# Folded weights interleaved on their way into PSUM, plain copies out, and a new order of all queues

## The chip, the cores and the metric

The kernel runs on one core of a Trainium2 chip. The time is that of one execution in microseconds of device time. A core has five queues of instructions that run side by side and wait for each other through semaphores: TensorE (PE, the matrix engine; its weight loads are shown as PEld), VectorE (DVE), ScalarE (ACT), GpSimd (POOL) and SyncE (SP, which here only issues DMAs).

## The reference

One block of a transformer on a sequence of 2048 rows of 448 numbers, in bf16: a linear attention with 16 heads of 28, then a gated feed forward with 1792 hidden units. Cut to what matters:

```python
x = A_x
xn = layernorm(x)
q, k, v = split_heads(xn @ wqkv)                  # 16 heads of 28
pq, pk = q @ w_phi[h], k @ w_phi[h]               # a 28x28 matrix per head
phi_q = concat(softmax(pq), softmax(-pq))
phi_k = concat(softmax(pk), softmax(-pk))
kv = phi_k.T @ v;  z = phi_k.sum(rows)
o  = (phi_q @ kv) / (phi_q @ z + 1e-6)
h  = x + heads_together(o) @ wo
hn = layernorm(h)
out = h + (sigmoid(hn @ w_gate) * (hn @ w_up)) @ w_down
```

## The kernel before

**Folding.** q is only used as q @ w_phi, and k as k @ w_phi. So the kernel multiplies the weights first: Wq2 = Wq @ w_phi and Wk2 = Wk @ w_phi, and projects the normalised rows with these. `fold(w, banks)` does it, with w = 0 for the keys and w = 1 for the queries, in four row tiles kt of 128 rows. One tile (`w2m0_0` to `w2m0_3`, `w2m1_0` to `w2m1_3`) is four matmuls of 112 columns, one for each group of four heads; together they fill 448 columns of a PSUM bank. `Wphi` holds w_phi as block diagonals, so that the columns of a group come out as head by head, 28 each. A copy (`w2e0_..`, `w2e1_..`) takes the bank to SBUF as bf16, on ACT or DVE. The key weights are transposed first on TensorE (`wT0` to `wT3`, taken out by `wTe0` to `wTe3`); the query weights arrive transposed by DMA (`ld_q0` to `ld_q3`).

**Interleaving.** Behind the projections, the sum over the 28 numbers of a head (`ss`, DVE) and the product with its reciprocal (`phi`) work on pairs of heads whose numbers alternate: number d of head 0, number d of head 1, number d+1 of head 0, and so on. The kernel before brings the weights' columns into this order in the copy: `w2e0` reads the bank with the two heads of a pair swapped to the innermost place, as one instruction of 448 columns, and `w2e1` does so in two instructions of 224 columns each, which also leave 8 columns of padding behind each 56.

**Stages.** The rows are 16 tiles t of 128. The loads `x0`, `x1`, `x2`, ... bring one or two tiles each. Statistics (`bst`, `agg`, DVE), the reciprocal root (`pow1`, POOL) and the normalisation (`xn`, on POOL, DVE or ACT) follow. The first four tiles are transposed on TensorE (`xT0` to `xT3`, copies `xT0e` to `xT3e`), the others by DMA from SP. Then:

- Key projections of the first four tiles `ppa0 ppb0 ppa2 ppb2` and value projections `vva0 vvb0 vva2 vvb2`, then both together for each further tile, `pva4 pvb4` to `pva15 pvb15`. Each is a pair: the contraction runs in two halves of 64 rows of the array that work at the same time, one on each of two banks, and in the b part the halves change banks. A b part that writes what its a part has just written waits for the end of the a part, and the order puts short items in between.
- `ek` (exponentials, two on ACT), `ss`, `rs` (reciprocal), `phi` (POOL or DVE), `v1` (the value copy, ACT or DVE), and the products `kva`, `kvb` of all 16 tiles, which add up in banks 6 and 7. `kvzA` to `kvzD` take them out.
- Query projections `pqa`, `pqb` for four chunks of 512 rows, exponentials `eq` on ACT.
- For each tile the numerator `num` (banks 6 and 7 again), and on DVE `rsm`, `qq`, `b`, `c`, `rden`; the division `o`; a transpose `oT`, on TensorE for tiles 0 and 1 and by DMA for the rest; the output projection (`wof0`, `wof1`, then `woa`, `wob` for two tiles at once); the residual `h` and the second normalisation (`bs2`, `ag2` or `nm`, `sq`, `ve`; `pow2`; `hn`) and its transpose `hT`, again on TensorE for tiles 0 and 1 (copies `hT0e`, `hT1e`).
- The feed forward in groups of 2, 2, 4, 4 and 4 tiles: gate and up `ga`, `gb` for each of 14 column tiles (256 columns for the first two groups, 512 for the others), the sigmoid `sig`, for some a copy `uc` of the up part (ACT), the product `hh` (DVE or POOL), and the down projections `dn`, `dp` in pairs of tiles, `dm`, `dl` for the last four. `fin` adds the residual, `out` stores.

Before the projections, TensorE runs matmuls on zeros (`warm0` to `warm9`).

**The order.** `ORDER` holds the whole order of all five queues, written out as names. The semaphores follow from the reads and writes that each item states: an item waits for the last writer of what it reads, and for the readers of what it overwrites. Each queue is worked off strictly in order. `PACE` holds back two loads until certain items are done. An item with a choice of engines runs on the engine in whose list it stands. Through the helper that records them most matmuls stand under line 333 in the profile, the fold's under 619, copies out of PSUM under 538, the query copies under 636.

Of the kernel before, what the change touches and what calls it, by code (L numbers as in the profile page):

```python
# [18 lines left out]
class Graph:  # L19
# [109 lines left out]
    def emit(self, nc):  # L129
# [133 lines left out]
    ),  # L263
# [86 lines left out]
def build(nc, A_x, A_wqkv, A_w_phi, A_wo, B_w_gate, B_w_up, B_w_down, out):  # L350
# [10 lines left out]
    with ExitStack() as es:  # L361
# [68 lines left out]
        def B(i):  # L430
            return ("bank", i)
# [180 lines left out]
        def fold(w, banks):  # L612
            for kt in range(KT):
# [3 lines left out]
                def mm(e, kt=kt, b=b, r0=r0):  # L617
                    for gg in range(G):
                        p = e.matmul(bk(b)[:, gg * GP:(gg + 1) * GP], lhsT=WT[w][:GP, gg, r0:r0 + P], rhs=Wphi[:, gg, :],  # L619
                                     start=True, stop=True)  # L620
                    return p
# [409 lines left out]
```

## Time and profile before

| | |
|---|---|
| median of 3 runs | 202.40 us (202.32 to 202.81) |
| the profiled execution | 202.64 us, its span 200.7 us |
| TensorE busy | 195.7 us (98%) |
| DVE / ACT / POOL busy | 129.1 / 100.0 / 64.5 us |
| granted TensorE clock | 1.0 |
| DMA | 16.25 MB moved, HBM read 8.34 MB |

The profile is one execution. Busy time of an engine is the union of its instructions; matmuls are pipelined and overlap, so the time from one start to the next is shorter than a duration. The timeline's rows give start, time covered, engine, line, output and inputs, and in brackets the idle time before, with what ended it. What lies between the span and the time of the execution (1.9 us) is outside the program's instructions.

### The profile page before, as it was taken

How to read it: one execution, taken by the hardware profiler on the slowest of the kernel's cores; microseconds unless marked ns; L12 is line 12 of the kernel's file. 1: busy time of each engine (PE TensorE's matmuls, PEld its weight loads, DVE VectorE, ACT ScalarE, POOL GpSimd, SP SyncE). 2: the span in 40 equal slices, each digit the busy share in tenths (PEclk: the TensorE clock that was granted, in tenths of full speed). 3: DMA queues.
4: the chain of work that ended last, by engine and by line, in shares of the span. 5: the costliest groups of instructions: out<-in, count | busy, mean ns of one | idle time of the engine just before them, and what ended most of it. 6: DMA issues, size and time to landing. Idle time of an engine off the chain costs nothing.

```text
span 200.7 us, 5879 instructions
## 1 busy us (share of the span) xinstructions
PE 195.7 (98%) x2500; PEld 115.2 (57%) x2500; DVE 129.1 (64%) x317; ACT 100.0 (50%) x215; POOL 64.5 (32%) x101
## 2 busy tenths in 40 slices
PE   7999999999989999999999999999999999999995
PEld 2945555666568878786444444555555555554443
DVE  6899999979899874445759877346332422272224
ACT  3778997998795874444342432324323212222220
POOL 5599989713534854560050110001400000000000
PEclk9999999999999999999999999999999999999999
DMA  6964442669997330221006320020212000004002
GB/s 163 311 143 99 83 82 52 178 200 285 322 188 96 78 57 9 46 56 31 0 10 117 78 45 11 20 60 23 56 49 54 0 0 3 0 0 140 0 0 91
DMA packets 32866, 16.25 MB, mean 81 GB/s; under 512 B 25096, under 2 KB 31944, under 8 KB 32840
## 3 DMA queue, kind: packets, MB, share of 16 engines
q1 hardware_dynamic: 32336, 15.86, 33.9%
q8 instruction: 19, 0.31, 0.6%
q10 hardware_dynamic: 504, 0.03, 0.2%
q14 instruction: 7, 0.06, 0.1%
HBM read 8.34 MB, written 1.84 MB: 51 GB/s over the span
## 4 chain that ended last, share of the span: by engine, by line
PE 97%; DVE 1%; issue 0%
PE psum L333 85%; PE psum L952 5%; PE psum L531 3%; PE psum L545 1%; PE psum L619 1%; PE psum L894 1%; PE psum L606 1%; DVE b_sb L810 0%; DVE c_sb L813 0%; PE psum L892 0%; DVE xnT L538 0%; DVE x_sb L959 0%; DVE zero L438 0%; DVE rsm L807 0%; DVE qq L808 0%
## 5 line engine op out<-in xcount | busy, mean ns | idle before, releaser
L333 PE MATMUL psum<-xnT,wg_sb 64*128 64x512 bf16 (+1 forms) x490 | 93.2, 333 | 0.1
L333 PE MATMUL psum<-xnT,wu_sb 64*128 64x512 bf16 (+1 forms) x490 | 92.7, 333 | 0.0
L919 ACT ACTIVATE sg_sb<-psum 128x512 bf16<-128x512 f32 (+1 forms) x70 | 35.5, 515 | 76.7 <-PE psum L333 76.1
L925 DVE TENSOR_TENSOR hhT<-sg_sb,psum 128x512 bf16<-128x512 bf16 (+1 forms) x44 | 28.9, 672 | 46.8 <-ACT sg_sb L919 46.5
L333 PEld LDWEIGHTS psum<-xnT,wg_sb 64*128 64x128 bf16 x490 | 44.5, 94 | 21.1 <-DVE hhT L925 2.2
L333 PEld LDWEIGHTS psum<-xnT,wu_sb 64*128 64x128 bf16 x490 | 44.5, 94 | 12.6
L333 PE MATMUL psum<-wd_sb,hhT 64*128 64x448 bf16 x336 | 37.0, 349 | 0.0
L333 PEld LDWEIGHTS psum<-wd_sb,hhT 64*128 64x128 bf16 x336 | 17.9, 94 | 14.2 <-DVE x_sb L845 0.5
L333 PE MATMUL psum<-wv_sb,xnT 64*128 64x448 bf16 x112 | 22.2, 351 | 0.1
L333 PE MATMUL psum<-Wk,xnT 64*128 64x448 bf16 x112 | 22.0, 350 | 0.1
L692 POOL TENSOR_TENSOR phi<-hhT,rs 128x896 bf16<-128x896 bf16 x10 | 17.6, 1765 | 2.5 <-DVE rs L688 2.1
L682 DVE TENSOR_REDUCE ss<-hhT 128x32 f32<-128x896 bf16 x16 | 17.2, 1073 | 0.5 <-ACT hhT L679 0.2
L854 POOL TENSOR_SCALAR ve<-ssq 128x1 f32<-128x1 f32 x11 | 2.7, 243 | 45.9 <-ACT junk L851 45.5
L730 ACT ACTIVATE eq<-psum 120x1024 bf16<-120x1024 f32 x16 | 15.6, 1029 | 1.4 <-PE psum L333 1.2
L333 PE MATMUL psum<-xnT,Wq 64*120 64x512 bf16 x112 | 14.9, 384 | 0.1
L819 POOL TENSOR_TENSOR o_pad<-c_sb,rden 128x448 bf16<-128x448 bf16 x10 | 9.3, 936 | 14.0 <-DVE rden L815 13.9
L924 ACT CAST xn_pad<-psum 128x256 bf16<-128x256 f32 x26 | 9.5, 378 | 5.6 <-PE psum L333 5.6
L959 DVE SCALAR_TENSOR_TENSOR x_sb<-psum,x_sb 128x448 bf16<-128x448 f32 (+2 forms) x17 | 9.4, 592 | 3.9 <-PE psum L333 2.1
L333 PE MATMUL psum<-wo_o,oT 64*128 64x448 bf16 x49 | 11.5, 349 | 0.0
L333 PE MATMUL psum<-wo_e,oT 64*128 64x448 bf16 x49 | 11.5, 349 | 0.0
L952 PE MATMUL psum<-wd_sb,hhT 128*128 128x448 bf16 (+2 forms) x70 | 11.1, 316 | 0.0
L333 PEld LDWEIGHTS psum<-Wk,xnT 64*128 64x128 bf16 x112 | 7.7, 94 | 5.3 <-issue 1.3
(113 smaller groups left out, 258.0 us busy)
## 6 DMA issues: line engine op xcount, KB each, us to landing
out_dram<-x_sb SPq DMA_DIRECT2D x15, 112.0 KB, 1.9
x_sb<-in_A_x_dram SPq DMA_DIRECT2D x7, 224.0 KB, 4.2
wd_sb<-in_B_w_down_dram SPq DMA_DIRECT2D x7, 224.0 KB, 5.5
wg_sb<-in_B_w_gate_dram SPq DMA_DIRECT2D x3, 448.0 KB, 5.5
wu_sb<-in_B_w_up_dram SPq DMA_DIRECT2D x3, 448.0 KB, 7.0
wv_sb<-in_A_wqkv_dram SPq DMA_DIRECT2D x2, 224.0 KB, 4.6
wk_sb<-in_A_wqkv_dram SPq DMA_DIRECT2D x2, 196.0 KB, 3.7
wo_e<-in_A_wo_dram SPq DMA_DIRECT2D x1, 336.0 KB, 3.0
```

The source lines that it names most:

```text
L333: p = e.matmul(o, lhsT=w, rhs=r, start=st, stop=sp, tile_position=(row, 0))
L531: p = e.matmul(bk(3)[:, 0:size], lhsT=zero[:, 0:P], rhs=zero[:, 0:size], start=True, stop=True)
L682: op("dve", "ss%d" % t, lambda e: e.tensor_reduce(ss[:, s, :].rearrange("p (b h) -> p b h", h=2), eks.rearrange("p b (d h) -> p b h d", h= ...
L692: return e.tensor_tensor(phi[:, sp, :, :, :].rearrange("p b a n -> p (b a) n")[:, :, 0:56].rearrange("p b (d h) -> p b d h", h=2), eks.rea ...
L730: op("act", "eq%d_%d%s" % (c, i, "pm"[sg]), lambda e, sg=sg: e.activation(eq[c][:, sg, 2 * i:2 * i + 2, :].rearrange("p g n -> p (g n)"), ...
L819: return e.tensor_tensor(o_pad[:, t % NO, off:off + D].rearrange("p (h d) -> p h d", h=H), c_sb[:, t % NS, :, 0:DH], rden[:, t % NS, :][:, ...
L854: op(("pool", "dve"), "ve%d" % t, lambda e: e.tensor_scalar(ve2[:, t:t + 1], ssq2[:, t:t + 1], 1.0 / D ** 3, EPS, op0=ALU.mult, op1=ALU.ad ...
L919: op("act", "sig" + nm, lambda e: e.activation(sg_sb[:, k, 0:N], bk(bg)[:, 0:N], ACT.Sigmoid), r=[B(bg)], w=[("sg", k)])
L924: op("act", "uc" + nm, lambda e: e.copy(up, bk(bu)[:, 0:N]), r=[B(bu)], w=[ub])
L925: op(("pool", "dve") if nm in UCOPY else "dve", "hh" + nm, lambda e: e.tensor_tensor(hhT[(t0 // 4) % NHH][:, ff, ns], sg_sb[:, k, 0:N], up ...
L952: p = e.matmul(bk(b)[:, lo:hi], lhsT=hb[:, ff, TS(t)], rhs=wd_sb[:, ff, lo:hi], start=ff == 0, stop=ff == FT - 1)
L959: op("dve", "fin%d%s" % (t, nm), lambda e: e.scalar_tensor_tensor(out=h_sb[:, t, lo:hi], in0=bk(b)[:, lo:hi], scalar=1.0, in1=h_sb[:, t, l ...
```

## The change

The fold's matmuls write their 112 columns with a step of two PSUM words: head 0 and head 1 of a pair are interleaved as they are written, and the moving operand is read in its stored order. Each copy then moves its bank in order, in one instruction, for keys and queries alike; only the padding of the query weights' target is left as a step. The columns that end up in SBUF are the same as before.

All five lists of `ORDER` are new. In SP's list `x12` stands ahead of three of the four query loads, `x14` one transpose later, `ld_wd3` ahead of `oT2` and `oT3`, `ld_wd4` to `ld_wd6` behind `oT7`. From DVE to ACT go `w2e0_1`, `w2e1_0` and `oT0e`, so that all eight weight copies are ACT's; from ACT to DVE go `xT2e`, `v1_4` and `h1`. DVE and POOL exchange products (`phi`, `hh`, `o`) and small items. On TensorE all items are there as before, in another order.

```diff
     "sp": (
-        "x1 x0 ld_k0 x2 ld_k2 x4 x6 ld_v0 x10 ld_v2 x8 ld_q2 ld_q1 ld_q0 x12 ld_q3 xT4 xT5 x14 xT6 ...
+        "x1 x0 ld_k0 x2 ld_k2 x4 x6 ld_v0 x10 ld_v2 x8 x12 ld_q1 ld_q2 ld_q0 ld_q3 xT4 xT5 xT6 x14 ...
-        "... ld_wd0 ld_wd1 ld_wd2 oT2 oT3 ld_wd3 ld_wd4 ld_wd5 ld_wd6 oT5 oT4 oT7 oT6 oT8 hT2 hT3 ...
+        "... ld_wd0 ld_wd1 ld_wd2 ld_wd3 oT2 oT3 oT4 oT5 oT6 oT7 ld_wd4 ld_wd5 ld_wd6 hT3 hT2 oT8 ...
     "act": (
-        "... wTe1 wTe0 xT1e xT0e w2e0_0 w2e0_2 w2e0_3 nm1_4 xT2e ek0 ek1 v1_0 par v1_1 ek2 w2e1_1 v1_2 v1_3 ek3 ...
+        "... wTe0 wTe1 xT1e xT0e w2e0_0 w2e0_2 w2e0_3 w2e0_1 nm1_4 ek1 ek0 nm1_6 v1_1 v1_0 ek2 nm1_8 w2e1_0 v1_2 ek3 ...
     "pe": (
-        "warm0 wT1 wT0 warm1 xT1 warm2 warm3 xT0 w2m0_0 wT2 wT3 warm4 warm5 w2m0_2 w2m0_1 w2m0_3 warm6 warm7 warm8 "
-        "ppa0 xT2 ppb0 xT3 warm9 vva0 vvb0 ppa2 seed ppb2 vva2 w2m1_1 vvb2 kvb0 w2m1_0 w2m1_3 pva4 kva0 kvb1 pvb4 "
+        "warm0 wT0 wT1 xT1 warm1 warm2 warm3 xT0 warm4 wT2 wT3 w2m0_0 warm5 w2m0_2 w2m0_1 w2m0_3 warm6 warm7 warm8 "
+        "warm9 ppa0 ppb0 vva0 xT3 xT2 vvb0 ppa2 seed ppb2 vva2 w2m1_0 vvb2 w2m1_2 w2m1_1 pva4 kva1 pvb4 pva5 kva0 "
...
-        "kvb15 kva14 pqa1_1 qs wwo num0 pqb1_1 num1 pqa2_0 num2 pqb2_0 pqa2_1 oT0 pqb2_1 num3 oT1 wof0 wof1 num4 "
-        "pqa3_0 pqb3_0 pqa3_1 num5 pqb3_1 hT0 hT1 wgu num6 ga0_1 ga0_0 gb0_1 gb0_0 woa2 num7 ga0_3 ga0_2 gb0_3 gb0_2 "
-        "wob2 num8 ga0_5 ga0_4 gb0_5 gb0_4 woa4 ga0_7 ...
+        "kvb14 kva15 pqa1_1 qs pqb1_1 wwo num0 pqa2_0 num1 pqb2_0 num2 pqa2_1 oT0 pqb2_1 pqa3_0 num3 oT1 wof0 wof1 "
+        "num4 pqb3_0 pqa3_1 pqb3_1 hT0 hT1 wgu num5 ga0_1 ga0_0 gb0_1 gb0_0 woa2 num6 ga0_3 ga0_2 gb0_3 wob2 gb0_2 "
+        "ga0_5 num7 gb0_5 ga0_4 gb0_4 ga0_7 ...
-        "wob12 gb4_10 ga4_13 dn4_0 ga4_12 gb4_13 gb4_12 dn4_4 ga8_1 ...
+        "wob12 gb4_10 ga4_13 gb4_13 ga4_12 dn4_0 gb4_12 dn4_4 ga8_1 ...
     "dve": (
-        "... bst1 agg1 bst0 xn1 agg0 xn0 bst3 bst2 agg3 wTe2 wTe3 agg2 bst5 w2e0_1 bst4 agg5 ... xT3e agg7 agg11 agg10 ss0 ...
+        "... bst1 agg1 bst0 agg0 xn1 xn0 bst3 bst2 agg3 wTe2 agg2 wTe3 bst4 bst5 nm1_2 bst7 agg5 ... xT3e xT2e ss1 bst8 ...
-        "... bs2_0 rden3 ag2_0 rsm4 bs2_1 qq4 ag2_1 b4 c4 hn0 hn1 rsm5 qq5 b5 hT0e c5 hT1e rden5 rsm6 ...
+        "... bs2_0 rden3 bs2_1 rsm4 ag2_0 ag2_1 qq4 h1 b4 hn0 hn1 c4 hT0e hT1e rden4 rsm5 qq5 b5 c5 rden5 ...
...
                 def mm(e, kt=kt, b=b, r0=r0):
                     for gg in range(G):
-                        p = e.matmul(bk(b)[:, gg * GP:(gg + 1) * GP], lhsT=WT[w][:GP, gg, r0:r0 + P], rhs=Wphi[:, gg, :],
+                        p = e.matmul(bk(b)[:, gg * GP:(gg + 1) * GP].rearrange("p (c d h) -> p c h d", c=2, h=2),
+                                     lhsT=WT[w][:GP, gg, r0:r0 + P], rhs=Wphi[:, gg, :].rearrange("p (c h d) -> p c h d", c=2, h=2),
                                      start=True, stop=True)
                     return p
...
                 if w == 0:
-                    dst = W2[0][:, kt, :].rearrange("p (c d h) -> p c h d", c=8, h=2)
-                    src = bk(b)[:, 0:D].rearrange("p (c h d) -> p c h d", c=8, h=2)
-                    evac("w2e%d_%d" % (w, kt), dst, src, B(b), ("W2", w, kt))
+                    dst, src = W2[0][:, kt, :], bk(b)[:, 0:D]
                 else:
                     dst = W2[1][:, kt, :, :].rearrange("p g (a n) -> p a g n", a=2)[:, :, :, 0:56]
-                    src = bk(b)[:, 0:D].rearrange("p (a g h d) -> p a g d h", a=2, g=G, h=2)
-
-                    def cp(m, dst=dst, src=src):
-                        def f(e):
-                            for a in range(2):
-                                p = m(e)(dst[:, a].rearrange("p g (d h) -> p g d h", h=2), src[:, a])
-                            return p
-                        return f
-                    op(("act", "dve"), "w2e%d_%d" % (w, kt), (cp(lambda e: e.copy), cp(lambda e: e.tensor_copy)), r=[B(b)], w=[("W2", w, kt)])
+                    src = bk(b)[:, 0:D].rearrange("p (a g n) -> p a g n", a=2, g=G)
+                evac("w2e%d_%d" % (w, kt), dst, src, B(b), ("W2", w, kt))
```

98 rows, old and new, of the table ORDER are left out of this document.

## The prediction, made before the changed kernel was run

> **What bounds the kernel now.** I read the busy shares first, then the chain that ended last, then the busy time by stretch, then the order of time around the two places where the stretches differ.
>
> ```profile
> span 200.7 us, 5879 instructions
> PE 195.7 (98%) x2500; PEld 115.2 (57%) x2500; DVE 129.1 (64%) x317; ACT 100.0 (50%) x215; POOL 64.5 (32%) x101
> PEclk9999999999999999999999999999999999999999
> PE 97%; DVE 1%; issue 0%
> ```
>
> TensorE (PE) is busy for 195.7 of 200.7 us at full granted clock, and the chain of waits is 97% TensorE. So this is a kernel whose end is the sum of TensorE's stream. The change adds and removes no matmul of the work, so it can move the time in three ways only: an earlier start of the stream, fewer or more holes in it, and matmuls that take longer. The stretches say where holes are left:
>
> ```profile
> 10.00:15.00 5.00, 4.94 (x51) 2.19 (x52) 4.98 (x16) 3.57 (x9) 4.89 (x10) 1.00 0.66 144
> 25.00:30.00 5.00, 5.00 (x76) 2.76 (x74) 5.00 (x10) 4.64 (x11) 4.41 (x5) 1.00 0.41 82
> 50.00:60.00 10.00, 8.98 (x144) 5.74 (x142) 9.14 (x29) 8.53 (x11) 4.10 (x6) 1.00 1.14 253
> 80.00:120.00 40.00, 40.00 (x531) 23.47 (x528) 26.22 (x71) 16.98 (x44) 10.38 (x19) 1.00 0.24 47
> ```
>
> The columns are the stretch, its length, then busy time of PE, PEld, VectorE (DVE), ScalarE (ACT), GpSimd (POOL). Visible holes: the start, 1.02 us in 50 to 60, the tail. From 80 to 120 there is none, so nothing done there on ACT, DVE or POOL can be gained. VectorE is as full as TensorE in 25 to 30: two engines go side by side, and work that leaves one of them does not shorten the stretch.
>
> **The copies out of PSUM.** These are the three kinds of copy, by line (min/median/max ns):
>
> ```profile
> L538 ACT CAST v<-psum x15: 535/541/604, 14.1 to 40.5; 128x448 bf16<-128x448 f32 x15
> L538 ACT CAST Wk<-psum x3: 662/664/664, 7.7 to 9.1; 128x448 bf16<-128x448 f32 x3
> L538 DVE CAST Wk<-psum x1: 641/641/641, 8.9 to 8.9; 128x448 bf16<-128x448 f32 x1
> L636 ACT CAST Wq<-psum x6: 346/377/401, 16.8 to 21.4; 128x224 bf16<-128x224 f32 x6
> ```
>
> The interleaving copy of a key weight costs 664 ns on ACT, a copy of the same size whose source is in order (the value tile v) 541; so the key copies (w2e0) lose 0.12 each. A query copy (w2e1) is two halves of 377, becomes one, and loses about 0.2. All eight now run on ACT, those of w2e0_1 and w2e1_0 and oT0e come from DVE, and DVE takes xT2e, v1_4 and h1 in return (copies of 0.4 to 0.6). That is nearly a swap for DVE, and worth time only where a copy is waited for: the start.
>
> ```profile
> 5.79 0.97 ACT L538 COPY WkT<-psum 112x448 bf16<-112x448 bf16 x2 [0.80 <-PE psum L606]
> 6.70 1.14 ACT L538 COPY xnT<-psum 128x512 bf16<-128x512 bf16 x2
> 7.74 0.66 ACT L538 CAST Wk<-psum 128x448 bf16<-128x448 f32 x1
> 8.57 1.19 ACT L538 CAST Wk<-psum 128x448 bf16<-128x448 f32 x2 [0.17 <-PE psum L619]
> 9.98 0.93 PE L333 MATMUL psum<-Wk,xnT 64*128 64x448 bf16 x8
> 10.85 0.40 PE L545 MATMUL psum<-ident,xn_pad 128*128 128x128 bf16 x4
> 11.18 0.74 PE L333 MATMUL psum<-Wk,xnT 64*128 64x448 bf16 x6
> 11.85 0.40 PE L545 MATMUL psum<-ident,xn_pad 128*128 128x128 bf16 x4
> 12.29 1.74 PE L333 MATMUL psum<-wv_sb,xnT 64*128 64x448 bf16 x14
> 13.95 0.93 PE L333 MATMUL psum<-Wk,xnT 64*128 64x448 bf16 x8
> 14.71 0.36 PE L716 MATMUL psum<-epsr,epsl 64*128 64x232 bf16 x2
> 17.46 0.97 ACT L538 CAST v<-psum 128x448 bf16<-128x448 f32 x2
> 18.14 0.35 PE L333 MATMUL psum<-Wk,xnT 64*128 64x448 bf16 x1
> ```
>
> The last key copy ends at 8.57 + 1.19 = 9.76 and the first projection (ppa0) starts at 9.98, 0.22 later. In the new order ACT makes four plain copies in a row. Two in a row take 0.97 (the row at 17.46), so they start 0.43 apart; from 7.74 the fourth starts at 9.03, ends at 9.57, and ppa0 starts at 9.79: **0.2 earlier**. What covers this is that the second normalised tile is ready sooner (agg0 stands ahead of xn1 on DVE) and wT2, wT3 ahead of the first fold on TensorE; without that cover the copies stretch as now and the gain is nothing.
>
> **The first pairs.** The b half of a pair writes the bank of its a half, so it waits for a's end unless something stands between. The 14 matmuls at 12.29 are vva0 and vvb0 with nothing between: 0.93 + 0.74 is nearly 1.74, so vvb0 starts 1.00 after vva0. With a filler the next item starts 0.76 after (13.95 to 14.71): a bare pair costs 0.24. Transposes in between cost 0.87 to enter (9.98 to 10.85), 0.33 for four. Now: ppa0, xT2, ppb0, xT3, vva0, vvb0, 3.97 from 9.98 to 13.95. New: ppa0 ppb0 bare 1.00, ppb0 0.57 (0.67 from 11.18 to 11.85, less the 0.11 that entering a transpose costs more), vva0 0.87, xT3 and xT2 together 0.33 + 0.22, vvb0 0.57: 3.56. But ppa2 needs both transposes evacuated, both now on DVE: xT3 starts 2.44 after ppa0, its copy starts about 0.43 later, two copies take 0.76, hand-over 0.12: 3.75. So **0.2 more** is gained, not 0.4.
>
> Then pva4 at 18.14 waits for the value copy, 17.46 + about 0.54 = 18.0. Everything ahead is 0.4 earlier, the query copy before it shorter, but its place behind ek2 and nm1_8 on ACT stays: I take 0.3. In return kvb0, 0.2 of TensorE, is not done yet by then. Left: 0.15.
>
> **18 to 43 us.** I take nothing. Both orders have four pairs with only one short kv item between (pva9, 11, 12, 14 now; pva4, 11, 12, 13 then), one place where two kv items of different halves meet, and three places where fold matmuls enter. TensorE has no hole to close, and DVE exchanges four phi products against four with POOL.
>
> On SP the load of x12 goes ahead of three weight transposes:
>
> ```profile
> 6.04 3.81 SPq L507 DMA_TRANSPOSE WqT<-in_A_wqkv_dram  x3
> 9.90 0.58 SPq L434 DMA_DIRECT2D x_sb<-in_A_x_dram  x1
> 10.53 1.12 SPq L507 DMA_TRANSPOSE WqT<-in_A_wqkv_dram  x1
> 16.38 0.37 PE L619 MATMUL psum<-Wphi,WqT 112*128 112x112 bf16 x4
> 51.40 4.70 SPq L832 DMA_TRANSPOSE oT<-o_pad  x2
> ```
>
> x12 starts 3.8 us earlier, three transposes 0.6 later, the fourth where it was (10.53), and its reader starts at 16.38: covered. x12's statistics move up with it on DVE, and nobody waited for them. Behind it, ld_wd3 is put ahead of oT2 and oT3, whose issue ends at 56.10, while their reader woa2 stands behind num5 or num6 and two gate/up items, past 58.4; and ld_wd4 to 6 go behind oT7, while their first reader dn0_8 stands behind nearly all gate/up items of the first two tiles. I take both at nothing; if that cover is gone the price is one more load's time, about 0.5.
>
> **43 to 59 us, the hole.**
>
> ```profile
> 43.84 1.24 DVE L759 TENSOR_TENSOR kvz<-psum,mask 64x232 bf16<-64x232 f32 x3 [1.06 <-PE psum L333]
> 45.19 0.41 PE L333 MATMUL psum<-kvz,eq 56*128 56x60 bf16 x16
> 45.41 0.85 PE L333 MATMUL psum<-xnT,Wq 64*120 64x512 bf16 x6
> 45.73 0.64 DVE L810 TENSOR_TENSOR b_sb<-psum,qq 128x464 bf16<-128x464 f32 x1
> 57.27 0.41 DVE L538 COPY xnT<-psum 128x512 bf16<-128x512 bf16 x1
> 57.60 0.63 DVE L813 TENSOR_TENSOR c_sb<-b_sb,psum 128x464 bf16<-128x464 bf16 x1
> 58.15 0.42 DVE L538 COPY xnT<-psum 128x512 bf16<-128x512 bf16 x1
> 58.38 0.40 PE L333 MATMUL psum<-kvz,eq 56*128 56x60 bf16 x16 [0.96 <-DVE c_sb L813]
> 122.72 0.92 PE L333 MATMUL psum<-wd_sb,hhT 64*128 64x448 bf16 x8
> 123.74 0.37 PE L333 MATMUL psum<-xnT,wg_sb 64*128 64x512 bf16 x1
> ```
>
> Here a DVE chain sets the end: kvz, b and c of each tile, two statistics, two normalisations (hn0, hn1), two copies (hT0e, hT1e), with c5 between the copies; num6 waits for that c5, hence 0.96 idle. The new order puts hT0e and hT1e together and c5 behind, which takes 0.63 out of the chain's end. It gives back at its head: num0 comes behind pqb1_1, 0.65 later (its 0.85 less the 0.2 by which items overlap), so b0, now at 45.73, waits until about 46.4; and h1 goes to DVE, about 0.55 (an estimate, by the 0.54 of a copy of its size), between the statistics and b4. pqa3_0, some 0.9 of TensorE by that row of six, moves ahead of num3, so less is left to hide the chain behind. Followed item by item by these durations, gate_up's first item comes some 0.4 earlier than now, but with num6 (0.22, from 45.19 to 45.41) still to do. Gain about 0.15; between a loss of 0.4 (h1 and num0 both fully in the chain, nothing absorbed) and a gain of 0.95 (the hole gone).
>
> **59 us to the end.** Two gate/up pairs become bare: ga0_4 gb0_4 (256 columns) and ga4_13 gb4_13 (512). By the price above 0.2 and 0.24. The second takes away a wait: ga8_1 starts at 123.74, 1.02 after the 8 matmuls before it, where 0.76 is the rule, because the last product of that bank was late; gb4_13 earlier frees it, 0.26 back. ga4_2 then has hardly any slack behind hh4_0 (b12 and c12 go ahead of it on DVE): 0.1. The closing down items only change places among themselves. Sum here: +0.3.
>
> **Sum.** At 18 us 0.15 gained, by 59 us 0.3, after it 0.3 lost: about 0, take +0.1 for the fold matmuls (below). The profiled execution took 202.64, its span 200.73 and 1.9 around it; it lies 0.24 above the median of the three runs, 202.40. So 202.7 for it, 202.5 against the median.
>
> **The unknown price: matmuls that write every second word.** No row of the trace shows one. The nearest is the fold itself, written in order: the 4 matmuls at 16.38 take 0.37 in all. Each lasts 0.21, so they start 0.05 apart. Lower bound: no change (the same matmul, same columns; nothing suggests a gain). Upper bound: a start every 0.10, were each word to take the time of two. I take 0.1 in all, being nearest to that row.
>
> **Rivals.** *The interleaved write halves the rate (slower).* 16 query-fold matmuls lie in the full stream: 16 x 0.05 = 0.8, of which pva4's wait can cover 0.2; the key folds delay the last two copies by about 0.2. Together +0.8 over my sum without the 0.1, 203.2. It is decisive from about 0.09 per start on. The trace can neither show nor exclude it. The Trainium skill, "PSUM — Partial Sum Buffer", section "Specifications (TRN2)", says that PSUM has 8-byte lines and any access pattern that is not contiguous slows matmuls significantly, which would make this the outcome, 203.2, where the row of the ordered fold gives 202.5. The pattern here has a step of exactly 8 bytes, and no run here shows it yet. Chance 0.28.
>
> *The hole closes (faster).* If the chain keeps its old head (num0's delay absorbed by DVE running ahead of the kv items) and loses c5 at its end, 0.7 to 0.95 of the 1.02 goes: 201.6. For it: DVE gives up three copies that are slow for their strided source and takes three plain ones, so phi15 may come sooner. Against: kvz cannot start before the last kv items, whose place in the stream is unchanged. Chance 0.22.
>
> *DVE's chain gets longer (slower).* b0 late by 0.65, h1 in the chain, oT1 behind pqa3_0 and num3: if TensorE has run out of pq items, 0.4 to 0.7 is lost at 50 to 60, with bank waits of 0.1 to 0.2 behind: 203.1. It decides if num0 starts later than about 45.9. Chance 0.16. My own case: 0.34.
>
> **How the numbers follow.** This kernel's measurement can tell about 0.3%, 0.6 us: faster is below 201.8, slower above 203.0. My case gives 0.1 faster, 0.8 same, 0.1 slower; the first rival 0.7 slower, 0.3 same; the second 0.8 faster, 0.2 same; the third 0.65 slower, 0.35 same. Sums: faster 0.21, same 0.45, slower 0.34. The range goes from the hole closed on top of the early gain (201.4) to both slow rivals with a late transpose (204.1). My own case alone: 202.0 to 203.0.
>
> **What would show it.** Right: ACT casts of Wk and Wq at about 540 ns each, no DVE cast of either; ppa0 at 9.8, ppa2 near 13.6, pva4 near 17.8; fold matmuls at 0.21 and 0.37 per four; the idle before num5 or the first gate item still 0.5 or more; ga8_1 0.76 behind its neighbour. Wrong: fold matmuls of 0.26 or more each (first rival); no idle of TensorE in 50 to 60 (second); gate_up's start after 58.9 (third). A slowdown made of small holes in 60 to 200, where I see only 0.3, would prove the count of bare pairs too short.

## The result: slower by 1.0%, outside the range

The changed kernel takes 204.74 us (median of 5 runs, 204.03 to 205.30), the kernel before 202.69 on the same chip: ratio 1.0103, 95% interval 1.0074 to 1.0132. The forecast was 202.5 with a range of 201.4 to 204.1; the result lies 0.64 above it. Two costs make up most of it: the stepped write (about 1.0 us), which was a rival, and a collision of two engines at `xn12` (0.5 us here, 0.7 to 0.8 with the old fold), which no case had.

The profiled execution took 205.09, its span 203.0. Its page, the engines' shares and the chain that ended last:

```profile
span 203.0 us, 5876 instructions
PE 197.2 (97%) x2500; PEld 114.9 (57%) x2500; DVE 126.5 (62%) x302; ACT 99.3 (49%) x212; POOL 75.3 (37%) x115
PE 88%; DVE 5%; DMA 2%; ACT 1%; SPq 1%; issue 1%
```

ScalarE and VectorE are less busy than before (GpSimd, which took over products, is 10.8 us busier), and the time went up. TensorE is busy 1.5 us longer with the same 2500 matmuls, and its part of the chain fell from 97% to 88%: some matmuls became longer, and other engines now set TensorE's time in places. The busy time by stretch of the changed kernel, columns as before:

```profile
10.00:15.00 5.00, 4.90 (x59) 2.73 (x58) 4.22 (x13) 3.01 (x8) 3.86 (x6) 1.00 1.12 150
25.00:30.00 5.00, 5.00 (x82) 2.93 (x79) 4.93 (x10) 3.96 (x10) 4.45 (x5) 1.00 0.52 57
50.00:60.00 10.00, 9.44 (x136) 5.33 (x134) 9.38 (x28) 8.69 (x11) 4.80 (x6) 1.00 1.12 265
80.00:120.00 40.00, 40.00 (x542) 25.38 (x538) 25.07 (x64) 17.30 (x47) 16.78 (x28) 1.00 0.24 50
```

The hole in 50 to 60 shrank from 1.02 to 0.56, and 80 to 120 is still full at full clock. So no hole in these stretches accounts for the loss. (A loss need not show as a hole: at the two bare pairs, in 65 to 68 and 121 to 124, TensorE counts as busy for 2.94 of 3.00.) Following TensorE's items by name through both traces gives these starts (us):

| | ppa0 | ppa2 | pva4 | pva11 | last kv item ends | first gate item | TensorE's end | span |
|---|---|---|---|---|---|---|---|---|
| before | 9.98 | 13.95 | 18.14 | 30.99 | 43.80 | 58.71 | 198.38 | 200.7 |
| changed | 11.24 | 15.01 | 19.55 | 33.30 | 46.00 | 59.92 | 200.46 | 203.0 |

1.3 us are lost before the first projection, 0.9 more between pva4 and pva11; 1.0 is won back between the last kv item and the first gate item, and 0.9 is lost behind it. The 1.3 is that of one execution, and a wait of 0.75 for a load, in the first row below, is part of it. The fold in the changed kernel, on TensorE and then on ScalarE, in order of time:

```profile
7.48 0.62 PE L606 MATMUL psum<-ident,wk_sb 112*112 112x112 bf16 x8 [0.75 <-DMA wk_sb<-in_A_wqkv_dram]
8.77 1.32 PE L619 MATMUL psum<-Wphi,WkT 112*128 112x112 bf16 x12
9.88 1.43 PE L531 MATMUL psum<-zero 128*128 128x128 bf16 x22
11.24 1.74 PE L333 MATMUL psum<-Wk,xnT 64*128 64x448 bf16 x14
8.52 0.53 ACT L538 CAST Wk<-psum 128x448 bf16<-128x448 f32 x1 [0.74 <-PE psum L619]
9.35 0.53 ACT L538 CAST Wk<-psum 128x448 bf16<-128x448 f32 x1 [0.30 <-PE psum L619]
10.12 0.97 ACT L538 CAST Wk<-psum 128x448 bf16<-128x448 f32 x2 [0.23 <-PE psum L619]
```

The copies became short, 0.53, but now wait for the fold each time: TensorE, not ScalarE, limits this chain. In the kernel before, the same twelve fold matmuls and the zero matmuls behind them stand so:

```profile
8.18 0.76 PE L619 MATMUL psum<-Wphi,WkT 112*128 112x112 bf16 x12
8.77 1.28 PE L531 MATMUL psum<-zero 128*128 128x128 bf16 x20
```

### The profile page after: what moved, and what is told of

It reads as the page before. It is cut to its first block, busy times and chain, and to the rows that moved or that the text cites. A ratio compares the mean times of both kernels' runs of the same rounds, so it can differ in the third digit from the quotient of the medians.

```text
span 203.0 us, 5876 instructions
## 1 busy us (share of the span) xinstructions
PE 197.2 (97%) x2500; PEld 114.9 (57%) x2500; DVE 126.5 (62%) x302; ACT 99.3 (49%) x212; POOL 75.3 (37%) x115
## 4 chain that ended last, share of the span: by engine, by line
PE 88%; DVE 5%; DMA 2%; ACT 1%; SPq 1%; issue 1%
PE psum L333 80%; PE psum L944 5%; DMA wk_sb<-in_A_wqkv_dram 2%; PE psum L619 2%; DVE ss L674 1%; DVE xn_pad L580 1%; SPq L434 1%; PE psum L531 1%; ACT hhT L670 1%; ACT hhT L671 1%; DVE c_sb L805 1%; DVE st L830 1%; DVE b_sb L802 0%; DVE hn_pad L852 0%; DVE xnT L538 0%
## 5 line engine op out<-in xcount | busy, mean ns | idle before, releaser
L333 PE MATMUL psum<-xnT,wg_sb 64*128 64x512 bf16 (+1 forms) x490 | 94.8, 333 | 0.3 <-DVE xnT L538 0.3
L333 PE MATMUL psum<-xnT,wu_sb 64*128 64x512 bf16 (+1 forms) x490 | 94.7, 333 | 0.1
L333 PE MATMUL psum<-wd_sb,hhT 64*128 64x448 bf16 x336 | 37.8, 349 | 0.0
L811 POOL TENSOR_TENSOR o_pad<-c_sb,rden 128x448 bf16<-128x448 bf16 x12 | 11.2, 936 | 29.0 <-DVE rden L807 29.0
L684 POOL TENSOR_TENSOR phi<-hhT,rs 128x896 bf16<-128x896 bf16 x10 | 17.0, 1705 | 4.3 <-DVE rs L680 2.6
L917 POOL TENSOR_TENSOR hhT<-sg_sb,xn_pad 128x256 bf16<-128x256 bf16 x16 | 10.7, 674 | 3.5 <-ACT xn_pad L916 1.7
L670 ACT ACTIVATE hhT<-psum 128x448 bf16<-128x448 f32 x16 | 8.8, 548 | 4.9 <-PE psum L333 4.7
```

The source lines that it names most:

```text
L333: p = e.matmul(o, lhsT=w, rhs=r, start=st, stop=sp, tile_position=(row, 0))
L670: e.activation(ek[:, s, :, 0, :], src, ACT.Exp)
L684: return e.tensor_tensor(phi[:, sp, :, :, :].rearrange("p b a n -> p (b a) n")[:, :, 0:56].rearrange("p b (d h) -> p b d h", h=2), eks.rea ...
L811: return e.tensor_tensor(o_pad[:, t % NO, off:off + D].rearrange("p (h d) -> p h d", h=H), c_sb[:, t % NS, :, 0:DH], rden[:, t % NS, :][:, ...
L917: op(("pool", "dve") if nm in UCOPY else "dve", "hh" + nm, lambda e: e.tensor_tensor(hhT[(t0 // 4) % NHH][:, ff, ns], sg_sb[:, k, 0:N], up ...
```

## The experiments

Times are medians; the kernel before had 202.6 to 202.7 beside each. Runs 1 to 4, 5 to 8, 9 to 12 and 13 to 14 were measured on four different chips, so a difference between runs of two of these sets leans on the kernel before being level on them (202.57 to 202.69). A kernel whose order is edited has line numbers some nine higher, because the lists are laid out anew.

### 1 and 2: one half of the change each

```diff
 # run 1: fold and copies of before, the new ORDER     # run 2: new fold and copies, ORDER of before
-ORDER = {...before...}                                -ORDER = {...new...}
+ORDER = {...new...}                                   +ORDER = {...before...}
```

> The new order of all queues, with the fold and its copies as before (matmuls write in order, copies interleave, 0.66 us for a key tile, two of 0.38 for a query tile). Write theory (writing every second PSUM word costs 0.045 us per fold matmul, 32 of them, 0.7 to 1.0 us of the 2.0 us lost): fold matmuls back at 0.21 us, and 203.7 to 204.0, a little of the gain eaten by the slower copies on ScalarE. Order theory (the order alone makes the loss): 204.5 or more, since the copies are only slower.

> The order of before, with the new fold and plain copies. Write theory: fold matmuls 0.30 us each, +0.7 to +1.0 us on the kernel before, 203.4 to 203.7. Order theory: no slower than the kernel before, 202.4 to 202.7, as the copies are shorter.

Run 1: 203.84, ratio 1.0063 (1.0043 to 1.0083). Run 2: 203.72, ratio 1.0064 (1.0037 to 1.0092). Each half is slower by itself, by 1.2 and 1.1 us. The fold's matmuls grouped by tile (min/median/max ns, first and last start), first of run 1, then of run 2:

```profile
L619 PE MATMUL psum<-Wphi,WkT x16: 209/212/214, 7.0 to 8.2; 112*128 112x112 bf16 x16
L619 PE MATMUL psum<-Wphi,WqT x16: 212/213/224, 16.0 to 22.1; 112*128 112x112 bf16 x16
```

```profile
L619 PE MATMUL psum<-Wphi,WkT x16: 256/301/301, 7.1 to 9.4; 112*128 112x112 bf16 x16
L619 PE MATMUL psum<-Wphi,WqT x16: 269/301/301, 17.1 to 21.9; 112*128 112x112 bf16 x16
```

With the order held, the stepped write takes a matmul of 112 columns from 213 to 301 ns. Twelve in a row take 1.31 in run 2 and 0.76 before: (1.31 - 0.30)/11 = 0.092 from start to start, where it was 0.050. This is what stands behind them in run 2:

```profile
8.35 1.31 PE L619 MATMUL psum<-Wphi,WkT 112*128 112x112 bf16 x12
9.46 1.32 PE L531 MATMUL psum<-zero 128*128 128x128 bf16 x20
10.71 0.93 PE L333 MATMUL psum<-Wk,xnT 64*128 64x448 bf16 x8
```

The folds of the keys stand in a row with nothing of the work between them, and the zero matmuls of warm6 to warm8 stand behind them in the same queue. From the end of the last fold to ppa0 there is 1.05 in run 2 (9.66 to 10.71) and 1.04 before (8.94 to 9.98). So all of their lengthening, 0.55 and 0.18 for the first four, comes out at ppa0: 0.73 later. From the start of the first fold to ppa0 the traces have 2.92 in the kernel before and in run 14, 3.66 in runs 2 and 8.

### 3, 4 and 8: where the step is, and which half of the folds pays

```diff
 # runs 3 (new order) and 4 (order of before): the step is in the moving operand, PSUM is written in order
-bk(b)[...].rearrange("p (c d h) -> p c h d", c=2, h=2), ... rhs=Wphi[:, gg, :].rearrange("p (c h d) -> p c h d", c=2, h=2)
+bk(b)[...].rearrange("p (c d h) -> p c d h", c=2, h=2), ... rhs=Wphi[:, gg, :].rearrange("p (c h d) -> p c d h", c=2, h=2)
 # run 8 (order of before): stepped write and plain copies for the keys only
+if w == 0: o, m = o.rearrange("p (c d h) -> p c h d", c=2, h=2), m.rearrange("p (c h d) -> p c h d", c=2, h=2)
```

> The new order and plain copies, but the interleaving is done on the moving operand: Wphi is read with a step of 28 elements and PSUM is written in order. Write theory: fold matmuls at 0.21 us, 203.5 to 203.9. Order theory: 204.5. If a stepped read of the moving operand is as slow as the stepped write, fold matmuls stay at 0.30 us and the time at 204.7.

> The order of before, plain copies, interleaving by the stepped read of the moving operand, PSUM written in order. Write theory: fold matmuls at 0.21 us, the projections start 0.1 to 0.3 us earlier, 202.2 to 202.7. Order theory: the same. If the stepped read is slow: as the second kernel of this set.

> The order of before, the stepped write and plain copies for the key weights alone (16 of 32 fold matmuls); the query weights as before. The full new fold in this order cost 1.1 us. If the fold of the keys stands in a row with nothing to hide it (its trace: the first projection 0.7 us later): +0.6 to +0.8, 203.2 to 203.4. If the prediction's step was right (0.2 us for the keys, the rest for the queries): +0.2 or less, 202.6 to 202.9.

Run 3: 204.39 (1.0091, 1.0061 to 1.0120). Run 4: 204.18 (1.0069, 1.0039 to 1.0098). Run 8: 203.20 (1.0027, 1.0014 to 1.0041). The rows of run 3, then of run 8:

```profile
L619 PE MATMUL psum<-Wphi,WqT x16: 257/260/272, 17.1 to 23.7; 112*128 112x112 bf16 x16
...
8.41 1.35 PE L619 MATMUL psum<-Wphi,WkT 112*128 112x112 bf16 x12
```

```profile
L623 PE MATMUL psum<-Wphi,WkT x16: 257/301/301, 7.1 to 9.4; 112*128 112x112 bf16 x16
L623 PE MATMUL psum<-Wphi,WqT x16: 212/213/223, 17.2 to 21.5; 112*128 112x112 bf16 x16
```

Runs 3 and 4 fell out otherwise than the plan of them: with PSUM written in order the matmul is not fast again. A read of `Wphi` that jumps by 28 elements makes it 260 ns, and the rate is as slow as with the stepped write, (1.35 - 0.26)/11 = 0.10. So these two runs do not acquit the write; they show that the same step costs as much on the reading side. What convicts the write is the pair of rows of run 8: in one execution, the matmuls that write with a step take 301 and those that write in order 213. Run 8 also divides the price. By the medians the keys' folds are 0.5 (203.20 against 202.69), the queries' the other 0.5 (203.72 against 203.20, on another chip). The traces are sharper, since they leave out how late the first fold starts: in the order of before the step adds 0.74 for the keys, between the first fold and ppa0, and 0.54 for the queries (4.57 for 4.19 from ppa2 to pva4, 25.82 for 25.66 from there to the end of the last kv item, in run 2).

### 5: VectorE and GpSimd at xn12

Run 1 left 1.2 us that belong to the order alone. Its TensorE waits once between 20 and 50 us, for a phi product. Here are VectorE and GpSimd of the changed kernel just ahead of that, and TensorE at the wait:

```profile
28.37 1.09 DVE L674 TENSOR_REDUCE ss<-hhT 128x32 f32<-128x896 bf16 x1
29.38 1.60 DVE L580 TENSOR_SCALAR xn_pad<-x_sb,mv,rst 128x512 bf16<-128x512 bf16 x1
30.90 1.07 DVE L674 TENSOR_REDUCE ss<-hhT 128x32 f32<-128x896 bf16 x1
29.15 1.68 POOL L684 TENSOR_TENSOR phi<-hhT,rs 128x896 bf16<-128x896 bf16 x1
33.06 0.40 PE L333 MATMUL psum<-v,phi 64*128 64x58 bf16 x16 [0.40 <-DVE phi L684]
```

The normalisation `xn12` takes 1.60; in the kernel before it takes 0.32. It begins 0.23 behind GpSimd's `phi6` and ends 0.15 after it (30.98 against 30.83). Run 1 has the same: 1.77 beside a `phi6` of 1.69. Behind `xn12` on VectorE come ss8, rs7, xn13 and phi7, and kvb7 on TensorE waits for phi7: 0.40 here, 0.72 in run 1. The first row is `xn12` in the kernel before, the other two are `xn12` and the wait in run 1:

```profile
26.14 0.32 DVE L580 TENSOR_SCALAR xn_pad<-x_sb,mv,rst 128x512 bf16<-128x512 bf16 x1
27.59 1.77 DVE L580 TENSOR_SCALAR xn_pad<-x_sb,mv,rst 128x512 bf16<-128x512 bf16 x1
31.43 0.40 PE L333 MATMUL psum<-v,phi 64*128 64x58 bf16 x16 [0.72 <-DVE phi L692]
```

Run 5 takes the two apart:

```diff
-"... ss5 agg15 ss6 rs5 agg13 agg14 phi5 rs6 ss7 xn12 ss8 ..."
+"... ss5 agg15 agg13 agg14 ss6 rs5 phi5 rs6 xn12 ss7 ss8 ..."
```

> The new order with the old fold, and on VectorE xn12 moved ahead of ss7, agg13 and agg14 ahead of ss6, so that xn12 runs before GpSimd starts phi6. Port theory (xn12 took 1.77 us in place of 0.32 because it started while GpSimd worked on phi6, and phi7 came 1.4 us late for that, which left TensorE idle 0.7 us before kvb7): xn12 at 0.3 to 0.5 us, no idle time before kvb7, 0.4 to 0.7 us faster than the same kernel without the move, 203.2 to 203.4. Rival (the hole at 31 us is filled later by the chain of 43 to 58 us, which waits for VectorE anyway): within 0.2 us of 203.8.

203.12, ratio 1.0023 (1.0005 to 1.0041): 0.7 below run 1. Its rows:

```profile
26.91 0.41 DVE L589 TENSOR_SCALAR xn_pad<-x_sb,mv,rst 128x512 bf16<-128x512 bf16 x1
27.02 1.85 POOL L701 TENSOR_TENSOR phi<-hhT,rs 128x896 bf16<-128x896 bf16 x1
```

`xn12` now begins first and takes 0.41, and it is GpSimd's product that stretches, 1.85 for 1.69. The wait of kvb7 is gone, pva11 starts at 30.94 (31.68 in run 1) and the last kv item ends at 43.73 (44.38); from pva4 to that end it is 25.78 in place of 26.58. The Trainium skill, "SBUF — State Buffer", section "Who interferes with whom", says that GpSimd shares one pair of ports with VectorE, that a VectorE instruction in a two-port mode, which tensor_scalar can enter, contends for it, that the first to issue holds the pair for its whole instruction, and that the other is blocked altogether. The end of `xn12` behind the end of `phi6`, and the reversal in run 5, agree with that.

### 6 and 7: the bare pairs filled again

```diff
-"... ga0_5 num7 gb0_5 ga0_4 gb0_4 ga0_7 ..."   "... ga4_13 gb4_13 ga4_12 dn4_0 ..."   "... out13 out12 ..."
+"... ga0_5 num7 ga0_4 gb0_5 gb0_4 ga0_7 ..."   "... ga4_13 ga4_12 gb4_13 dn4_0 ..."   "... out12 out13 ..."
 # run 7: the edit of run 5 as well
```

> The new order with the old fold, and the two bare gate/up pairs filled (ga0_4 ahead of gb0_5, ga4_12 ahead of gb4_13), and out12 stored ahead of out13. Theory of bare pairs (0.25 and 0.23 us each by the trace): 0.4 to 0.5 us faster than without, 203.3 to 203.4, with up to 0.1 more from the stores. Rival (a filled pair brings back the bank wait that the bare one removed): within 0.2 us of 203.8, with a wait at ga8_1 or ga0_7.

> Both of the above. If the two losses add up and are what the order costs, 0.9 to 1.2 us faster than the new order with the old fold: 202.6 to 203.0, level with the kernel before. If something else in the order costs the rest: above 203.2. If the earlier start of the stream in this order counts in full: 202.2.

Run 6: 204.94 (1.0123, 1.0096 to 1.0151), 1.1 slower than run 1. Run 7: 204.52 (1.0083, 1.0064 to 1.0102), 1.4 slower than run 5. My theory, that the bare pairs are a loss to be undone, falls. TensorE's waits behind 60 us in run 6:

```profile
PE psum L342 <- DVE hhT L934: 0.8, 2, 0.6
PE psum L342 <- ACT sg_sb L928: 0.4, 1, 0.4
```

Run 1 has no wait there. Taking the next item's bank earlier meets the product (hhT) or the sigmoid (sg_sb) of the tile that still holds it. The bare pair costs its 0.2, but it is placed where the other choice costs up to 0.6.

### 9: the collision taken out of the changed kernel itself

The edit of run 5, made to the changed kernel.

> The changed kernel whole (stepped write, new order), with one thing moved: on VectorE, xn12 is put two items later, behind phi5 and rs6, and agg13, agg14 ahead of ss6, so that GpSimd does not run a phi product while it runs. If the shared port (VectorE's xn12 held up by GpSimd's phi6) is what delays phi7 and the kv item behind it, the same 0.7 as with the old fold comes off: xn12 0.3 to 0.4 us in place of 1.6, pva11 near 32.5 in place of 33.3, about 204.0. If the stepped write has moved the two engines against each other so that another wait is behind it, or if the gain with the old fold was only chance of the landings, it stays within 0.3 of 204.7.

204.24, ratio 1.0073 (1.0056 to 1.0090): 0.5 below the changed kernel, where 0.7 was expected. The expectation calls `xn12` two items later; in the list it stands one item earlier, ahead of ss7. The two intervals overlap (the changed kernel has 1.0074 to 1.0132), but the traces give the same size: from pva4 to the end of the last kv item 25.98 in place of 26.46. `xn12` takes 0.31, pva11 starts at 32.36. The write's price here, against run 5, is 1.1, net of the plainer copies.

### 10, 11 and 12: the new order before the gate stage, the old one behind it

```diff
 # run 10, old fold: each list of run 5 up to num5, wgu, hT0e, hT1e, then the list of before, but
-"... num6 ga0_1 ga0_0 gb0_1 gb0_0 woa2 num7 ..."
+"... ga0_1 ga0_0 num6 gb0_1 gb0_0 woa2 num7 ..."
 # run 11: run 10 with "w2m0_0 wT2 wT3" for "wT2 wT3 w2m0_0"      # run 12: run 10 with the new fold
```

> Old fold (written in order, copies interleave). Order: up to num5, wgu and the evacuations of hT0, hT1 the new order with xn12 moved as above; from the first gate/up item on the order of the kernel before, with num6 two items later than there (behind ga0_0), because its c5 is now behind the two copies. If the new order is better before 59 us and worse behind it by the 0.65 us of the gate/up stage and the 0.2 of the tail, gate_up starts near 57.7 and TensorE ends 139.9 later, near 197.6: about 202.1, below the kernel before (ratio near 0.997). If the lost time behind 59 us comes from what the new order owes at that point (late exponentials, late products) and not from its order behind it, the 0.65 stays: about 202.9.

> As the hybrid, with the first fold (w2m0_0) put back ahead of wT2 and wT3 on TensorE. If the place of the two transposes exposes the landing of the second key load, the wait before wT2 has 0.3 of work ahead of it again: up to 0.3 less where the load lands after 7.2 us, and less spread among the runs. If not, the same time as the hybrid within 0.1.

> As the hybrid, with the changed kernel's fold: PSUM written with a step of two words, plain copies. If the stepped write has a price of its own (0.7 to 0.8 at the start, 0.4 to 0.5 among the query folds, less the plainer copies' 0.14 to 0.2), it is 0.9 to 1.1 above the hybrid in any order, near 203.1. If the new order with its plain copies was made so as to hide it, less than 0.4.

Run 10: 203.39 (1.0036, 1.0022 to 1.0051), where 202.1 was expected of a better early order. TensorE in run 10 around the first gate item (57.57):

```profile
56.91 0.40 PE L342 MATMUL psum<-kvz,eq 56*128 56x60 bf16 x16 [0.24 <-DVE c_sb L822]
59.21 0.40 PE L342 MATMUL psum<-kvz,eq 56*128 56x60 bf16 x16 [0.42 <-DVE c_sb L822]
61.52 0.40 PE L342 MATMUL psum<-kvz,eq 56*128 56x60 bf16 x16 [0.50 <-DVE c_sb L822]
```

The gate stage begins 1.1 earlier than before, with num6 (0.22) still to do, and num6 and num7 then wait for the products c5 and c6: 0.92 together, beside the 0.96 of the one wait that the kernel before had there. The hole was moved, not closed: putting c5 behind hT1e leaves the same products to VectorE, and only an order that puts num6 and num7 later, as the new one does, keeps part of the gain.

Run 11: 203.73 (1.0056, 1.0037 to 1.0074), not less than run 10. I had argued, from TensorE's 0.75 wait for `wk_sb` in the changed kernel's profile, that wT2 and wT3 ahead of the first fold expose that load. Run 11 shows that the old place is no gain in the median, but not that the load stays hidden. With the first fold in front, wT2 starts 0.65 after its load has landed (6.51, 7.16); the trace puts the idle 0.61 ahead of that fold down to the load of `Wphi`. With wT2 in front, as in the change, it starts within 0.05 of the landing in the traces of runs 1, 5, 6, 7 and 13, and the landing lies anywhere from 6.09 to 7.27. ppa0 comes 3.3 to 3.5 behind it: at 9.47 to 10.59, in kernels whose lists are the same up to there, where the kernel before has 9.98 and run 14, with the same start on TensorE, 10.18. So the new place wins when the load is early and loses when it is late.

Run 12: 204.40 (1.0086, 1.0067 to 1.0104), 1.0 above run 10, as the theory of a price of its own said.

### 13: other fillers

```diff
-"... gb0_5 ga0_4 gb0_4 ga0_7 woa4 gb0_7 ga0_6 wob4 ..."   "... ga4_13 gb4_13 ga4_12 dn4_0 gb4_12 dn4_4 ga8_1 ..."
+"... gb0_5 ga0_4 woa4 gb0_4 ga0_7 ga0_6 gb0_7 wob4 ..."   "... ga4_13 dn4_0 gb4_13 ga4_12 dn4_4 gb4_12 ga8_1 ..."
 # on top of run 5; out12 ahead of out13 too
```

> Old fold, new order with xn12 moved, and the two bare gate/up pairs filled without taking a bank earlier: woa4 stands between ga0_4 and gb0_4 (wob4 then behind gb0_7), dn4_0 between ga4_13 and gb4_13, dn4_4 between ga4_12 and gb4_12; out12 is put ahead of out13. If the rest of the new order's loss behind 59 us is the price of the bare pairs (0.22 and 0.23) and of the order of the last stores (0.1 to 0.2), first gate item to TensorE's end goes from 140.5 to about 140.1 and the time to about 202.6, level with the kernel before. If the loss is the late products and exponentials that the new order owes at 59 us, the waits come back at other items, as in the first attempt to fill the pairs: 203.0 or more.

205.80, ratio 1.0151 (1.0130 to 1.0172), 2.7 above run 5: the worst of all. TensorE's waits of run 13 from 60 to 130:

```profile
PE psum L342 <- DVE x_sb L854: 1.1, 1, 1.1
PE psum L342 <- DVE hhT L934: 0.4, 2, 0.2
PE psum L342 <- ACT xn_pad L933: 0.3, 1, 0.3
```

dn4_0 one item earlier needs a bank that the residual sum (line 854) has not emptied yet: 1.1 for a bare pair of 0.23. The second reading of its expectation held at these three places: the waits came back at other items. Of the 2.7, 1.8 lie in the span (202.8 against 201.0 in the median). The other 0.9 lie outside it, 3.1 in place of 2.1; no trace shows what they are.

### 14: the same ports in the kernel before

```diff
-"... ident pow1_1 phipad opad0 pow1_0 nm1_3 pow1_3 nm1_2 ..."   "... phi12 phi13 o0 ..."
+"... ident pow1_1 pow1_0 nm1_3 pow1_3 phipad nm1_2 ..."         "... phi12 phi13 opad0 o0 ..."
```

> The kernel before with two fills moved on GpSimd: phipad behind pow1_3, opad0 behind phi13. In the kernel before xn1 on VectorE takes 0.88 us while these fills run; its neighbour xn0, with GpSimd idle, 0.41. If GpSimd's work holds up VectorE's normalisation whatever the work is, xn1 takes 0.41, xn0 starts 0.4 earlier, and ppa0 comes 0.0 to 0.2 earlier (ScalarE's copies are the limit from there): 202.5 against 202.7. If the 0.88 has another cause (its operand has just been written), it stays 0.88 and the time is the same.

202.52 against 202.57, ratio 0.9993 (0.9982 to 1.0003): no difference that can be told. `xn1` in the kernel before, with the first and the last of GpSimd's three fills beside it, and then in run 14:

```profile
4.34 0.88 DVE L580 TENSOR_SCALAR xn_pad<-x_sb,mv,rst 128x512 bf16<-128x512 bf16 x1
4.25 0.53 POOL L468 MEMSET phi<- 128x512 bf16 x1
4.86 0.22 POOL L466 MEMSET o_pad<- 128x128 bf16 x1
```

```profile
4.39 0.40 DVE L589 TENSOR_SCALAR xn_pad<-x_sb,mv,rst 128x512 bf16<-128x512 bf16 x1
```

A fill, which reads nothing, holds the normalisation up as a product does: `xn1` ends 0.14 behind the last fill (5.22, 5.08). Here it costs no time: `xn0` starts 0.43 earlier in run 14, but ppa0 does not (10.18, before 9.98). No version is measurably faster than the kernel before.

## Why the prediction was wrong, step by step

The step that failed first is the price of the stepped write, put at 0.1 where it is about 1.05; the second is the stretch from 18 to 43 us, put at nothing where 0.6 was lost.

Along one row of kernels the medians differ so: before to run 5, +0.4 (the rest of the order); run 5 to run 9, +1.1 (the stepped write); run 9 to the changed kernel, +0.5 (`xn12`). Such differences add up to the whole, 2.05, whatever their causes, so the sum proves nothing. What can be compared with the prediction term by term are the stretches of the traces: from pva4 on, a stretch has the same length to 0.02 in every trace in which its order and its fold are the same (us; the last column is the median time of an execution outside its span):

| | first fold to ppa0 | to ppa2 | to pva4 | to the end of the last kv item | to the first gate item | to TensorE's end | to the span's end | outside |
|---|---|---|---|---|---|---|---|---|
| before | 2.92 | 3.97 | 4.19 | 25.66 | 14.91 | 139.67 | 2.35 | 1.80 |
| run 2 | 3.66 | 3.97 | 4.57 | 25.82 | 14.91 | 139.67 | 2.35 | 1.80 |
| run 1 | 2.81 | 3.76 | 4.19 | 26.58 | 13.92 | 140.54 | 2.53 | 2.05 |
| run 5 | 2.80 | 4.25 | 4.19 | 25.78 | 13.92 | 140.53 | 2.54 | 2.10 |
| run 9 | 3.31 | 3.76 | 4.54 | 25.98 | 13.91 | 140.54 | 2.54 | 2.11 |
| changed | 3.31 | 3.76 | 4.54 | 26.46 | 13.92 | 140.54 | 2.53 | 2.09 |

The changed row less the row of before comes to 1.7. The other 0.4 of the 2.05 lies ahead of the first fold or is scatter (an estimate, by difference); the landing of the load named under run 11 varies by more than that (6.09 to 7.27).

**The unknown price of the stepped write: wrong by about 1.0.** I took 0.1 in all; the table has 1.05 (run 9 against run 1 up to pva4, against run 5 behind it). The reason that I gave was "being nearest to that row". That row was of the matmul without the step; it could set the lower end, and it was no evidence about the other. All 32 matmuls run at about 0.09 from start to start, close to the upper bound of 0.10. The first rival was the outcome for the fold. The Trainium skill, "PSUM — Partial Sum Buffer", section "Specifications (TRN2)", says that a pattern that is not contiguous slows matmuls significantly. The runs agree: 213 to 301 ns at a step of exactly 8 bytes. The rival's sum of 0.8 was still small. The queries' half was right (0.6 expected, 0.55 in the table), the keys' half was not (0.2 expected, 0.50 in the new order, 0.74 in the old one): I thought of the keys' folds as feeding copies that ScalarE limits, and did not follow that the folds stand in a row, with 20 zero matmuls queued behind them ahead of ppa0.

**18 to 43 us, "I take nothing": wrong by 0.6 in the changed kernel, by 0.9 with the old fold.** I counted TensorE's items and VectorE's load, and found an exchange of four products against four. What I did not look at is what each of VectorE's normalisations has beside it on GpSimd. The trace of before had the sign: two runs of the same instruction, `xn1` at 0.88 and `xn0` at 0.41, 1.6 us apart. In run 1, where only the order is new, pva4 starts 0.34 earlier than before and the last kv item ends 0.58 later; of these 0.92 run 5, with `xn12` moved, has 0.12 left (25.78 from pva4 to the last kv item, 25.66 before). In the changed kernel moving `xn12` takes off 0.48.

**The first pairs: right; ppa0 itself: luck.** From ppa0 to ppa2 run 1 and the changed kernel take 3.76, where 3.75 was written, and 3.97 before. Run 1 also has ppa0 at 9.84, ppa2 at 13.61 and pva4 at 17.80, where 9.79, near 13.6 and 17.8 were written down. But ppa0 lies between 9.47 and 10.59 in five traces of that same start, so one agreement shows no earlier start. When it is as early as in run 5 (9.50), ppa2 waits and the 0.2 of the pairs is lost again (4.25). What the plain copies were to bring is not there either: run 1 kept the interleaving ones, 2.36 for four in a row, and in the changed kernel the copies took the expected 0.53 and waited. The 0.15 that the prediction has left at pva4 is 0.3 less 0.2, so 0.1.

**43 to 59 us: the gain was five times what I wrote.** This stretch takes 0.99 less than before in every kernel with the new order, 0.77 when num6 (0.22), still to do, is counted; 0.15 was written. Run 1 reaches the first gate item at 58.30, 0.4 earlier than before, as said, but only because the 0.92 lost ahead of it hides most of this gain: luck. In size the outcome is the second rival's, though the hole did not close (and one of the three copies that this rival calls slow for their source, oT0e, is a plain one). In the changed kernel the hole is these two waits, 0.5 in place of 0.96; where the rest of the gain comes from was not followed:

```profile
59.26 0.40 PE L333 MATMUL psum<-kvz,eq 56*128 56x60 bf16 x16 [0.24 <-DVE c_sb L805]
59.92 0.27 PE L333 MATMUL psum<-xnT,wg_sb 64*128 64x256 bf16 x1 [0.26 <-DVE xnT L538]
```

The sign that I had named for the third rival, a gate stage later than 58.9, shows here and would have misled: it starts at 59.92 because everything ahead is late, not because that chain is longer. A sign should be a difference within its stage, not a time since the start.

**59 us to the end: the right direction, half the size.** From the first gate item to TensorE's end run 1 takes 140.54 and the kernel before 139.67, 0.87 more, of which 0.22 is num6: +0.65 where +0.3 was written. The two bare pairs cost 0.22 and 0.23 and the wait of ga8_1 went, as said. Not foreseen were 0.17 at ga0_1 and 0.15 at num6, two items that start slowly behind a chain which has only just delivered; behind TensorE's end the last stores add 0.18 (2.53 to the end of the span, 2.35 before; with out12 ahead of out13, in runs 6, 7 and 13, 2.29 to 2.30).

**Outside the span: taken as unchanged, 0.3 more.** I put 1.9 around the span for both kernels. The kernel before and runs 2, 4, 8, 10, 12 and 14, which have its order behind 59 us, lie at 1.80 to 1.82 in the median, the changed kernel and runs 1, 3, 5, 6, 7 and 9 at 2.02 to 2.13. That is most of what run 5 still loses against the kernel before. But run 11, which has the old order there too, lies at 2.09; the cause stays open.

**The moves on SP: nothing found.** From 10 us on no load stands in the list of TensorE's waits of the changed kernel. They were not tried by themselves.

## What to carry to other kernels

The steps tried here in a matmul's output and in its moving operand cost 0.04 to 0.05 us per matmul of 112 columns, on the engine that bounds this kernel; a copy that interleaves is paid for on ScalarE, which had slack. So before moving a layout change from a copy into a matmul, ask which of the two engines waits. A new order that looks neutral by counts of work per engine can still lay two instructions side by side that hold each other up: go through the neighbours of each normalisation on the other engine, and distrust any instruction that has two durations in one trace. And a pair that looks badly placed in a tuned order is to be priced against the bank that its cure would need. Compare stretches between named items, not times since the start: a late load moves every later time, and two errors can cancel in one.

## What the runs showed of the hardware that I had not expected

- A stepped read of the moving operand (28 elements) slows the matmul's rate as much as a stepped write does (0.10 and 0.09 from start to start, 0.05 in order), though the single matmul looks shorter, 260 against 301 ns.
- GpSimd's fills of memory hold up VectorE's normalisation too (0.88 beside three fills, 0.40 without them), not only a product that reads (1.60 to 1.77, 0.31 to 0.41 without it).
